# Sparse-expert slots of a fused attention and MoE kernel: who computes the weight splits, who scales the result, and in which order

## The chip, the cores and the metric

The kernel runs on one core of one Trainium2 chip. The metric is the device time of one execution in microseconds (us). TensorE is written PE, its weight loads PEld, VectorE DVE, ScalarE ACT, GpSimd POOL and SyncE SP. A "q" behind a name (POOLq) is that engine's sequencer, which issues DMAs, counts semaphores and branches. SBUF is the on-chip memory, PSUM the memory that PE writes to.

## The reference

Three stages follow one another: a decayed causal attention, a dense mixture of experts (every token through all 8 experts, weighted by a balanced table P), and a sparse mixture (every token through the one expert with the largest logit).

```python
def reference(**kw):
    attn_out = _attn_ref(q, k, v)                       # 4 x 8 heads x 576 x 64
    x = attn_out.transpose(0, 2, 1, 3).reshape(2304, 512)
    x = _moe_ref(x, moe_w_gate, moe_w1, moe_w2)         # dense, E = 8, F = 1024
    return _moe2_ref(x, moe2_w_gate, moe2_w1, moe2_w2)  # sparse

def _moe2_ref(x, w_gate, w1, w2):
    logits = x @ w_gate
    expert_idx = np.argmax(logits, axis=1)
    gate_w = softmax(logits)[np.arange(N), expert_idx]
    for e in range(8):
        mask = expert_idx == e
        h = np.maximum(x[mask] @ w1[e], 0.0)            # w1[e]: 512 x 1024
        out[mask] = gate_w[mask, None] * (h @ w2[e])    # w2[e]: 1024 x 512
```

All is float32. The kernel multiplies on PE in a reduced 32-bit format (fp32r) and keeps accuracy by splitting each operand into a high part `hi` (the value rounded to fp32r) and a low part `lo = value - hi`; one product is then three matmuls: hi·hi, hi·lo and lo·hi.

## The kernel before

Attention takes the first 330 us, the dense experts run until about 1695 us, and the rest is the sparse stage, class `Top1`, which the change is about. It sorts the tokens by expert and works in **slots** of 128 rows of one expert. There are up to 26 slots (NSLOT); 18 of them (NFULL) run always, slots 18 to 25 stand each under its own guard `tc.If(n > t)`. In the profiled execution 22 slots run, 0 to 21, and four guards are skipped. Slots 0 and 1 are woven by hand into the routing arithmetic of `build`; slots 2 to 21 are calls of `slot(t)`, each 48 products of 128x512 columns on PE and three groups of four transposes.

One expert's weights are eight **units** of 128x1024: units 0 to 3 are rows of w1, units 4 to 7 pieces of w2. A unit c lands by an SP transfer of 512 KB in the tile `raws[c]` (only where the next slot's expert differs), and `split(c)` makes its two halves: ACT copies raw to hi (op0h to op6h, u7h), then lo = raw - hi (op0l to op6l, u7l) is computed, for c = 3 and 7 on POOL, for the others on DVE. The split is done anew for every slot, changed expert or not.

The work of a slot t, in the order in which it is written:

- `gather(t + 2)`: POOL fetches 128 rows of a later slot by an indirect DMA into `xg`.
- `hidden(t, 0)` and `hidden(t, 1)`: 12 products each on PE (tile phs) of the row's transposed halves xth, xtl with units 0 to 3; after each, two splits of units 4 to 7 and `relu` on ACT (tile hrow).
- the SP loads of units 4 to 7 for slot t + 1.
- `th(0)`, `tx(t + 1)`, `th(1)`: three groups of four PE transposes in a row. `th` transposes half of the hidden rows (pth; ACT writes hth, DVE htl); `tx` transposes the next slot's token rows (ptx; ACT writes xth, DVE xtl).
- `result`: 24 products (tile pys) of hth and htl with units 4 to 7.
- the splits of units 0, 1, 3, 2 for slot t + 1, and the loads of units 0 to 3 for slot t + 2 (`ahead`).
- `finish`: o = pys * gate on DVE (L1325), then POOL writes the 128 rows to their places in the output by an indirect DMA (L1328).

ACT, DVE and PE run their instructions in the written order; for SP and POOL a scheduler chooses the order. Each engine works through its own queue in order and waits at the head for what its next instruction needs. Two results, o0 and o1 of slots 0 and 1, are kept unscaled (`keep`, L1318) until the gates are known; the function `mid` scales and writes them within slot 2.

Of the kernel before, what the change touches and what calls it, by code (L numbers as in the profile page):

```python
# [15 lines left out]
AF = mybir.ActivationFunctionType  # L16
ALU = mybir.AluOpType
# [20 lines left out]
def split_lo(eng, out, src, hi):  # L38

    return eng.tensor_tensor(out=out, in0=src, in1=hi.bitcast(F32), op=ALU.subtract)  # L40
# [336 lines left out]
def drain(gen):  # L377

    while True:
        try:  # L380
            next(gen)
        except StopIteration as s:
            return s.value
# [95 lines left out]
def token_tasks(nc, X, ops, lo_engs):  # L479
# [18 lines left out]
    def sub(out, a, b):  # L498
# [4 lines left out]
    b11, b12, b21, b22 = (0, 0), (1, 0), (0, 1), (1, 1)  # L503
    return [
        split(B11, *b11), split(B21, *b21), sub(b11, b12, b11),
        sub(b12, b22, b12),
        split(B22, *b22), sub(b22, b22, b11), split(T2, *b22),
        split(T1, *b11), split(T3, *b12), sub(b21, b21, b22), split(T4, *b21),
    ]

# [241 lines left out]
MANUAL = {mybir.EngineType.Activation, mybir.EngineType.DVE, mybir.EngineType.PE}  # L752
NSLOT = 26
NFULL = NT
# [397 lines left out]
class Top1:  # L1152
# [58 lines left out]
    def unit(self, c):  # L1211
        return self.units[c]

    def split(self, c, eng=None):
        hi, lo = self.unit(c)
        self.nc.scalar.activation(hi, self.raws[c], AF.Copy)  # L1216
        if eng is None:
            eng = self.nc.gpsimd if c in (3, 7) else self.nc.vector
        split_lo(eng, lo, self.raws[c], hi)

    def xt(self, t):
        return tuple(x[:, t % 2] for x in self.xts)
# [41 lines left out]
        nc.scalar.activation(hi[:, gs, :], pt, AF.Copy)  # L1264
        split_lo(nc.vector, lo[:, gs, :], pt, hi[:, gs, :])

    def result(self, hi, lo, py=None, gs=range(2)):
        if py is None:
            py = self.pyp.tile([128, DM], F32, name="pys", tag="py")
        n = 12 * gs[0]  # L1270
        for g in gs:
            fcs = range(4 * g, 4 * g + 4)
            w = {fc: [x[:, 512 * (fc % 2):512 * (fc % 2) + 512] for x in self.unit(4 + fc // 2)]
                 for fc in fcs}
            mm = [(hi, fc, w[fc][i]) for fc in fcs for i in range(2)]
            mm += [(lo, fc, w[fc][0]) for fc in fcs]
            for a, fc, ww in mm:
                self.nc.tensor.matmul(py, a[:, fc, :], ww, start=n == 0, stop=n == 23)
                n += 1
        return py  # L1280

    def slot(self, t, mid=None):
        h, hi, lo = self.begin()
        if t + 2 < NSLOT:
            self.gather(t + 2)
        for f in range(2):
            ph = self.hidden(t, f)
            for c in (4 + 2 * f, 5 + 2 * f):
                self.split(c)
            self.relu(f, ph, h)  # L1290
        if t + 1 < NSLOT:
            if t >= NFULL:
                self.regs_of(t + 1)
            for c in range(4, 8):
                self.load(t + 1, c)
        self.th(0, h, hi, lo)
        if t + 1 < NSLOT:
            self.tx(t + 1, self.ptp, "pt")
        self.th(1, h, hi, lo)
        if mid:  # L1300
            mid()
        py = self.result(hi, lo)
        if t + 1 < NSLOT:
            for c in (0, 1, 3, 2):
                self.split(c)
        self.ahead(t + 2)
        self.finish(t, py)

    def ahead(self, t):
        if t < NSLOT:  # L1310
# [10 lines left out]
    def finish(self, t, py, o=None):  # L1321
        nc = self.nc
        if o is None:
            o = self.op.tile([128, DM], F32, name="o", tag="o")
        nc.vector.tensor_scalar(  # L1325
            out=o, in0=py, scalar1=self.res["gate"][:, t:t + 1], scalar2=None, op0=ALU.mult
        )
        nc.gpsimd.indirect_dma_start(  # L1328
            out=self.out,
            out_offset=bass.IndirectOffsetOnAxis(ap=self.res["sidx"][:, t:t + 1], axis=0),  # L1330
            in_=o, in_offset=None, bounds_check=N - 1, oob_is_err=False,
        )
# [3 lines left out]
def build(ctx, tc, q, k, v, moe_w_gate, moe_w1, moe_w2, moe2_w_gate, moe2_w1, moe2_w2,  # L1336
          c_gk, c_gq, c_row, out):
    nc = tc.nc
# [88 lines left out]
    gs = ExitStack()  # L1427
# [24 lines left out]
    with tc.manual_schedule(engines=order):  # L1452
# [3 lines left out]
        for u in range(2 * E):  # L1456
# [20 lines left out]
            if u == 2 * E - 1:  # L1477
# [8 lines left out]
                g, w = nc.gpsimd, nc.vector  # L1486
# [24 lines left out]
        t1 = None  # L1511
        for n, u in enumerate(range(2 * E - 1, -1, -1)):
# [8 lines left out]
            else:  # L1521
# [3 lines left out]
                t1 = Top1(tc, ctx, ident, x2d, moe2_w1, moe2_w2, res, out, list(ops), raws, aux)  # L1525
# [38 lines left out]
    with tc.manual_schedule(engines=MANUAL):  # L1564
        t1.gather(1)
        t1.split(7)
        ro.v.bg = [ro.gates(0, tmp)]
        h0, h1 = t1.begin(), t1.begin()

        ph = t1.hidden(0, 0, None, range(0, 2))  # L1570
        next(lp)
        ph = t1.hidden(0, 0, ph, range(2, 4))
        drain(lp)
        t1.relu(0, ph, h0[0])
        ro.choose(1, tmp)
        ro.v.bg.append(ro.gates(1, tmp))
        ph = t1.hidden(0, 1, None, range(0, 1))
        ro.count(1)
        t1.hidden(0, 1, ph, range(1, 4))
        t1.relu(1, ph, h0[0])  # L1580
        ro.totals(1)
        ro.slots(tmp)
        t1.th(0, *h0)
        t1.th(1, *h0)
        t1.tx(1, t1.ptp, "pt")
        py = t1.result(*h0[1:])
        ro.experts(tmp)
        t1.ahead(2)
        o0 = t1.keep(0, py)

        ro.ranks(1)
        ro.slots_of(tmp)
        ph = t1.hidden(1, 0)
        t1.relu(0, ph, h1[0])
        ph = t1.hidden(1, 1)
        t1.relu(1, ph, h1[0])
        ro.onehot(tmp)
        ro.rows(tmp)
        for t in (2, 3):
            t1.gather(t)  # L1600
        t1.th(0, *h1)
        t1.th(1, *h1)
        for c in range(4):
            t1.split(c)
        py = t1.result(*h1[1:], None, range(0, 1))
        t1.tx(2, t1.ptp, "pt")
        t1.result(*h1[1:], py, range(1, 2))
        for c in range(4, 8):
            t1.load(2, c)
        ro.v.rest()  # L1610
        t1.ahead(3)
        o1 = t1.keep(1, py)
        rg = ro.row_gates(tmp)
        next(rg)

        def mid():
            drain(rg)
            t1.finish(0, o0, o0)
            t1.finish(1, o1, o1)

        for t in range(2, NFULL):
            t1.slot(t, mid if t == 2 else None)
    n = nc.values_load(
        res["nslot"][0:1, 0:1], min_val=NFULL, max_val=NSLOT,
        skip_runtime_bounds_check_because="18 to 26 slots hold 2304 tokens of 8 experts",
    )
    for t in range(NFULL, NSLOT):
        with tc.If(n > t):
            with tc.manual_schedule(engines=MANUAL):
                t1.slot(t)  # L1630


def consts():
# [33 lines left out]
```

## Time and profile before

| | |
|---|---|
| time, median of 3 runs (lowest to highest) | 2002.8 us (2002.36 to 2005.55) |
| the profiled execution's own time | 2002.13 us |
| its span in the trace | 2000.3 us |
| mean granted clock of PE, share of full speed | 0.996 |
| busy share of PE, DVE, ACT, POOL over the span | 98%, 63%, 42%, 15% |
| start of slot 2, start of slot 3, last product of slot 21 | 1725.91, 1738.87, 1986.94 us |

Times in the trace count from the start of the span; 1.8 us of the execution lie outside it. A row of a timeline gives start, duration, engine, line of the kernel, operation, the tile written, the tiles read, the shape, and in brackets how long the engine had been idle before it and what ended that. A product (MATMUL) is listed with 0.39 us, but products overlap: their starts follow one another every 0.23 us.

### The profile page before, as it was taken

The page shows a single profiled execution, that of the slowest core. Times are in us where ns is not written, and L with a number is a line of the kernel's source. Part 1 is how long each engine was busy: PE and PEld are TensorE (multiplying, and loading weights), DVE is VectorE, ACT ScalarE, POOL GpSimd, SP SyncE. Part 2 cuts the span into 40 slices and gives each one's busy share as a digit, 9 for nine tenths or more (in the row PEclk, how much of TensorE's full clock was granted, in tenths as well). Part 3 has the DMA queues.
Part 4 walks back from the last instruction along what each step waited for, and adds up shares of the span by engine and source line. Part 5 has one row for each costly group of instructions (what it writes and reads, how often), then busy time and mean ns, then how long its engine had stood idle before and what let it go on. Part 6 is the DMA issues. An engine that isn't in the chain of part 4 may idle for free.

```text
span 2000.3 us, 25444 instructions
## 1 busy us (share of the span) xinstructions
PE 1956.9 (98%) x9584; PEld 1627.4 (81%) x9584; DVE 1252.1 (63%) x2059; ACT 847.7 (42%) x1454; POOL 298.9 (15%) x250
## 2 busy tenths in 40 slices
PE   8989999999999999999999999999999999999997
PEld 7777888888888888888878888888878888777775
DVE  7897565555555555555455556555576654988886
ACT  6665424232222233323333333333333334577785
POOL 6572000000000000000000000000000001465654
PEclk9999999999999999999999999999999999999998
DMA  5621111111111110111311111111111113112755
GB/s 132 142 61 64 42 43 43 43 43 43 43 42 43 43 37 28 42 43 43 111 33 64 43 43 64 42 54 52 43 46 60 47 59 116 43 43 77 249 200 192
DMA packets 112111, 134.94 MB, mean 67 GB/s; under 512 B 62190, under 2 KB 62446, under 8 KB 111600
## 3 DMA queue, kind: packets, MB, share of 16 engines
q1 hardware_dynamic: 106960, 121.92, 19.0%
q0 software_dynamic: 3680, 11.02, 1.7%
q8 instruction: 77, 1.26, 0.3%
q10 hardware_dynamic: 1344, 0.33, 0.1%
q14 instruction: 50, 0.41, 0.1%
HBM read 182.53 MB, written 12.58 MB: 98 GB/s over the span
## 4 chain that ended last, share of the span: by engine, by line
PE 82%; DVE 8%; ACT 5%; issue 3%; DMA 1%; POOL 0%; SPq 0%; ACTq 0%; POOLq 0%; DVEq 0%
PE pyt L731 37%; PE pha L609 17%; PE phc L609 8%; PE phr L706 5%; PE phb L609 4%; PE phs L1250 4%; DVE op2l L40 2%; PE po L274 2%; PE ps L210 1%; ACT op3h L1216 1%; PE pS L236 1%; ACT op2h L1216 1%; PE rpl L832 1%; DMA raw<-in_moe_w_dram 1%; PE pgate L1381 1%
## 5 line engine op out<-in xcount | busy, mean ns | idle before, releaser
L731 PE MATMUL pyt<-w2hi,hhi 128*128 128x512 f32 x1024 | 402.5, 393 | 2.4 <-DVE xb L742 2.2
L731 PE MATMUL pyt<-w2hi,hlo 128*128 128x512 f32 x1024 | 398.9, 390 | 0.0
L731 PE MATMUL pyt<-w2lo,hhi 128*128 128x512 f32 x1024 | 398.5, 389 | 0.0
L635 ACT ACTIVATE q<-pha 128x512 f32<-128x512 f32 x192 | 114.7, 599 | 266.8 <-PE pha L609 264.4
L623 ACT ACTIVATE hhi<-q 128x512 fp32r<-128x512 f32 x192 | 121.4, 632 | 249.9 <-DVE q L631 249.9
L731 PEld LDWEIGHTS pyt<-w2hi,hhi 128*128 128x128 f32 x1024 | 192.3, 188 | 42.8 <-DVE xb L742 2.9
L731 PEld LDWEIGHTS pyt<-w2hi,hlo 128*128 128x128 f32 x1024 | 192.2, 188 | 40.7
L731 PEld LDWEIGHTS pyt<-w2lo,hhi 128*128 128x128 f32 x1024 | 192.4, 188 | 38.8
L624 DVE SCALAR_TENSOR_TENSOR hlo<-q,hhi 128x512 fp32r<-128x512 f32 x192 | 133.0, 693 | 96.8 <-ACT hhi L623 90.8
L742 DVE SCALAR_TENSOR_TENSOR xa<-pyt,P,xa 128x512 f32<-128x512 f32 x140 | 105.0, 750 | 136.0 <-PE pyt L731 135.2
L742 DVE SCALAR_TENSOR_TENSOR xb<-pyt,P,xb 128x512 f32<-128x512 f32 x120 | 90.1, 751 | 94.0 <-PE pyt L731 94.0
L631 DVE TENSOR_TENSOR q<-phb,q 128x512 f32<-128x512 f32 x64 | 44.3, 692 | 166.0 <-PE phb L609 166.0
L40 POOL TENSOR_TENSOR op2l<-xb,op2h 128x1024 fp32r<-128x1024 f32 x1 | 2.4, 2387 | 719.4 <-ACT op2h L494 719.4
L631 DVE TENSOR_TENSOR q<-phc,q 128x512 f32<-128x512 f32 x128 | 87.8, 686 | 34.0 <-PE phc L609 33.1
L561 ACT ACTIVATE w3h<-raw 128x512 fp32r<-128x512 f32 x31 | 19.6, 631 | 160.4 <-DVE raw L567 160.3
L567 DVE TENSOR_TENSOR raw<-raw 128x512 f32<-128x512 f32 x124 | 85.1, 687 | 1.1
L40 DVE TENSOR_TENSOR w2lo<-raw,w2hi 128x512 fp32r<-128x512 f32 x124 | 84.6, 683 | 0.0
L587 ACT ACTIVATE w2hi<-raw 128x512 fp32r<-128x512 f32 x124 | 77.1, 623 | 0.0
L714 DVE SCALAR_TENSOR_TENSOR rlo<-phr,rhi 128x512 fp32r<-128x512 f32 x32 | 22.1, 691 | 87.7 <-ACT rhi L713 87.7
L908 POOL TENSOR_SCALAR Bm<-c,ro 128x128 bf16<-128x128 bf16 x2 | 1.3, 653 | 456.2 <-DVE ro L408 456.2
L561 ACT ACTIVATE w4h<-raw 128x512 fp32r<-128x512 f32 x31 | 19.6, 632 | 116.2 <-DVE raw L567 116.2
L40 DVE TENSOR_TENSOR op2l<-raw,op2h 128x1024 fp32r<-128x1024 f32 x22 | 60.6, 2756 | 10.1 <-ACT op2h L1216 9.6
(391 smaller groups left out, 4765.3 us busy)
## 6 DMA issues: line engine op xcount, KB each, us to landing
raw<-in_moe_w_dram SPq DMA_DIRECT2D x180, 512.0 KB
raw<-in_moe_w_dram SPq DMA_DIRECT2D x62, 1024.0 KB
kt<-in_k_dram SPq DMA_DIRECT2D x32, 128.0 KB
vt<-in_v_dram SPq DMA_DIRECT2D x32, 128.0 KB
qt<-in_q_dram SPq DMA_DIRECT2D x32, 128.0 KB
x2d<-xa SPq DMA_DIRECT2D x10, 256.0 KB
xbd<-xb SPq DMA_DIRECT2D x1, 2048.0 KB
xb<-xbd SPq DMA_DIRECT2D x2, 1024.0 KB
```

The source lines that it names most:

```text
L40: return eng.tensor_tensor(out=out, in0=src, in1=hi.bitcast(F32), op=ALU.subtract)
L567: nc.vector.tensor_tensor(out=q(*out), in0=q(*a), in1=q(*b), op=op)
L587: nc.scalar.activation(hi, self.raw2[:, fc, :], AF.Copy)
L609: self.nc.tensor.matmul(bank, ww[:, k, 128 * p:128 * p + 128], xx[:, k, :], start=start and n == 0, stop=stop and n == 5, skip_group_check ...
L623: nc.scalar.activation(hi, c, AF.Relu)
L624: nc.vector.scalar_tensor_tensor(out=lo, in0=c, scalar=0.0, in1=hi.bitcast(F32), op0=ALU.max, op1=ALU.subtract)
L631: self.nc.vector.tensor_tensor(out=s, in0=p, in1=s, op=ALU.add)
L635: self.nc.scalar.activation(t, c, AF.Copy)
L706: nc.tensor.matmul(pt[:, j, :], w[:, k, 128 * j:128 * j + 128], xr[x][:, xi, k, :], start=n == 0, stop=n == 11,)
L731: nc.tensor.matmul(pt, hh, ww, start=n == 0, stop=n == 11)
L742: nc.vector.scalar_tensor_tensor(out=acc, in0=pt, scalar=P[:, i, e:e + 1], in1=acc, op0=ALU.mult, op1=ALU.add)
L1250: nc.tensor.matmul(ph, xx[:, k, :], ww[:, fs], start=n == 0, stop=n == 11)
```

## The change

Five things are changed, all in the sparse stage.

1. The low halves of all eight units are computed on DVE; POOL computes none.
2. `finish` scales on ACT instead of DVE, for o0 and o1 in slot 2 as well.
3. `slot` is written in another order: the transposes are spread among the products (th(0) in the middle of the second hidden half, tx behind it, th(1) after eight result products), the splits of units 0 to 5 for the next slot are spread over the slot, and the splits of units 6 and 7 open the next one. The loads follow: 4 and 5 at the slot's start, 6 and 7 behind their splits.
4. In `build`, the loads of units 4 to 7 for slot 2 and its splits 4 and 5 stand earlier.
5. The guards of slots 18 to 25 are nested: the guard of slot t + 1 stands inside the body of slot t.

```diff
-    def split(self, c, eng=None):
+    def split(self, c):
         hi, lo = self.unit(c)
         self.nc.scalar.activation(hi, self.raws[c], AF.Copy)
-        if eng is None:
-            eng = self.nc.gpsimd if c in (3, 7) else self.nc.vector
-        split_lo(eng, lo, self.raws[c], hi)
+        split_lo(self.nc.vector, lo, self.raws[c], hi)
...
     def slot(self, t, mid=None):
         h, hi, lo = self.begin()
+        nxt = t + 1 < NSLOT
         if t + 2 < NSLOT:
             self.gather(t + 2)
-        for f in range(2):
-            ph = self.hidden(t, f)
-            for c in (4 + 2 * f, 5 + 2 * f):
-                self.split(c)
-            self.relu(f, ph, h)
-        if t + 1 < NSLOT:
+        if nxt:
             if t >= NFULL:
                 self.regs_of(t + 1)
-            for c in range(4, 8):
+            for c in (4, 5):
                 self.load(t + 1, c)
+        ph = self.hidden(t, 0)
+        for c in (6, 7):
+            self.split(c)
+            if nxt:
+                self.load(t + 1, c)
+        self.relu(0, ph, h)
+        ph = self.hidden(t, 1, None, range(0, 2))
+        if nxt:
+            self.split(0)
         self.th(0, h, hi, lo)
-        if t + 1 < NSLOT:
+        self.hidden(t, 1, ph, range(2, 4))
+        if nxt:
+            self.split(1)
+        self.relu(1, ph, h)
+        if nxt:
+            self.split(2)
             self.tx(t + 1, self.ptp, "pt")
+        py = self.result(hi, lo, None, slice(0, 8))
         self.th(1, h, hi, lo)
         if mid:
             mid()
-        py = self.result(hi, lo)
-        if t + 1 < NSLOT:
-            for c in (0, 1, 3, 2):
-                self.split(c)
+        if nxt:
+            self.split(3)
+        self.result(hi, lo, py, slice(8, 24))
+        if nxt:
+            self.split(4)
+            self.split(5)
+        self.finish(t, py)
         self.ahead(t + 2)
-        self.finish(t, py)
...
-        nc.vector.tensor_scalar(
-            out=o, in0=py, scalar1=self.res["gate"][:, t:t + 1], scalar2=None, op0=ALU.mult
-        )
+        nc.scalar.activation(o, py, AF.Copy, scale=self.res["gate"][:, t:t + 1])
...
         t1.ahead(2)
+        for c in range(4, 8):
+            t1.load(2, c)
         o0 = t1.keep(0, py)
...
-        py = t1.result(*h1[1:], None, range(0, 1))
+        py = t1.result(*h1[1:], None, slice(0, 12))
+        t1.split(4)
         t1.tx(2, t1.ptp, "pt")
-        t1.result(*h1[1:], py, range(1, 2))
-        for c in range(4, 8):
-            t1.load(2, c)
+        t1.result(*h1[1:], py, slice(12, 24))
+        t1.split(5)
...
-    for t in range(NFULL, NSLOT):
-        with tc.If(n > t):
-            with tc.manual_schedule(engines=MANUAL):
-                t1.slot(t)
+    def further(t):
+        if t < NSLOT:
+            with tc.If(n > t):
+                with tc.manual_schedule(engines=MANUAL):
+                    t1.slot(t)
+                further(t + 1)
+
+    further(NFULL)
```

On DVE one whole slot reads as follows before, from the split of unit 6 on (raw_101 to raw_13812 are the tiles of the landed weights, two units in each of the first two):

```order
L40 TENSOR_TENSOR op6l<-raw_13811,op6h 128x1024
L40 TENSOR_TENSOR htl<-pth,hth 128x512
L40 TENSOR_TENSOR xtl<-ptx,xth 128x512
L40 TENSOR_TENSOR htl<-pth,hth 128x512
L40 TENSOR_TENSOR op0l<-raw_101,op0h 128x1024
L40 TENSOR_TENSOR op1l<-raw_101,op1h 128x1024
L40 TENSOR_TENSOR op2l<-raw_102,op2h 128x1024
L1325 TENSOR_SCALAR o<-pys,gate 128x512
L40 TENSOR_TENSOR op4l<-raw_13809,op4h 128x1024
L40 TENSOR_TENSOR op5l<-raw_13810,op5h 128x1024
```

and this is the same stretch of DVE's queue with the change:

```order
L40 TENSOR_TENSOR op6l<-raw_13811,op6h 128x1024
L40 TENSOR_TENSOR u7l<-raw_13812,u7h 128x1024
L40 TENSOR_TENSOR op0l<-raw_101,op0h 128x1024
L40 TENSOR_TENSOR htl<-pth,hth 128x512
L40 TENSOR_TENSOR op1l<-raw_101,op1h 128x1024
L40 TENSOR_TENSOR op2l<-raw_102,op2h 128x1024
L40 TENSOR_TENSOR xtl<-ptx,xth 128x512
L40 TENSOR_TENSOR htl<-pth,hth 128x512
L40 TENSOR_TENSOR op3l<-raw_102,op3h 128x1024
L40 TENSOR_TENSOR op4l<-raw_13809,op4h 128x1024
L40 TENSOR_TENSOR op5l<-raw_13810,op5h 128x1024
```

The two splits of POOL have come in, the scaling of the result has gone, and the splits now stand between the small ones.

On PE, this is the passage from the hidden products to the result products of one slot before:

```order
L1250 MATMUL phs<-op3h,xtl 128x512
L1262 MATMUL pth<-ident,hrow 128x128 x4
L1229 MATMUL ptx<-ident,xg_13815 128x128 x4
L1262 MATMUL pth<-ident,hrow 128x128 x4
L1278 MATMUL pys<-op4h,hth 128x512
```

and with the change, from the middle of the second hidden half to the ninth result product:

```order
L1248 MATMUL phs<-op1h,xtl 128x512
L1260 MATMUL pth<-ident,hrow 128x128 x4
L1248 MATMUL phs<-op2h,xth 128x512
L1248 MATMUL phs<-op2l,xth 128x512
L1248 MATMUL phs<-op2h,xtl 128x512
L1248 MATMUL phs<-op3h,xth 128x512
L1248 MATMUL phs<-op3l,xth 128x512
L1248 MATMUL phs<-op3h,xtl 128x512
L1227 MATMUL ptx<-ident,xg_13815 128x128 x4
```

The three groups of transposes stood together and now stand apart, each behind products; the third (second half of the hidden rows) follows eight result products further on.

On POOL the queue ends before with these instructions for the last guard (the ISA row counts up the semaphores of the slot's transfers where the slot is skipped):

```order
L1628 COMPARE_AND_BRANCH
L40 TENSOR_TENSOR u7l<-raw_13812,u7h 128x1024
L1328 DMA out_dram<-o,sidx 2304x512
L1628 UNCONDITIONAL_BRANCH
L1628 ISA
L1628 UNCONDITIONAL_BRANCH
```

and with the change with these:

```order
L1642 COMPARE_AND_BRANCH
L1339 DMA out_dram<-o,sidx 2304x512
L1642 COMPARE_AND_BRANCH
L1339 DMA out_dram<-o,sidx 2304x512
L1642 UNCONDITIONAL_BRANCH
L1642 ISA
L1642 UNCONDITIONAL_BRANCH
L1642 ISA
```

A skipped guard was followed by the next guard, with an ISA row of its own for each; now the skipped branches stand one behind the other at the end of the program, each followed by a jump past the rest, so that one of them is run.

## Rows read from the trace of the kernel before

**Rows 1.** Busy us by window: span, PE, PEld, DVE, ACT, POOL, PEclk, DMA share, GB/s.

```profile
1940.00:1960.00 20.00, 19.67 (x98) 16.05 (x97) 16.86 (x17) 17.27 (x23) 12.01 (x7) 1.00 0.95 329
```

**Rows 2.** Chain that ended last, two steps: start, duration, engine, tile, line.

```profile
1921.31 2.89 DVE op2l L40
...
1934.32 2.88 DVE op2l L40
```

**Rows 3.** Waits from 1720 us on: total us, times, longest us.

```profile
PE phs L1250 <- DVE op2l L40: 7.5, 19, 1.2
...
ACT op5h L1216 <- DMA raw<-in_moe_w_dram: 2.0, 3, 1.0
```

**Rows 4.** Timeline at the start of slot 14, PE, DVE and POOL.

```profile
1881.38 2.68 POOL L40 TENSOR_TENSOR op3l<-raw,op3h 128x1024 fp32r<-128x1024 f32 x1 [1.41 <-ACT op3h L1216]
...
1882.28 2.88 DVE L40 TENSOR_TENSOR op2l<-raw,op2h 128x1024 fp32r<-128x1024 f32 x1 [0.48 <-ACT op2h L1216]
...
1884.48 0.39 PE L1250 MATMUL phs<-op2h,xth 128*128 128x512 f32 x1
...
1885.21 0.50 PE L1250 MATMUL phs<-op2l,xth 128*128 128x512 f32 x1 [0.34 <-DVE op2l L40]
...
1885.54 0.39 PE L1250 MATMUL phs<-op2h,xtl 128*128 128x512 f32 x1
...
1885.77 0.40 PE L1250 MATMUL phs<-op3h,xth 128*128 128x512 f32 x1
```

**Rows 5.** Timeline of the same slot: two groups of transposes, ACT's copy of the first.

```profile
1889.20 0.60 PE L1262 MATMUL pth<-ident,hrow 128*128 128x128 f32 x4
...
1889.64 0.60 PE L1229 MATMUL ptx<-ident,xg 128*128 128x128 f32 x4
...
1889.89 0.59 ACT L1264 ACTIVATE hth<-pth 128x512 fp32r<-128x512 f32 x1
```

**Rows 6.** Timeline of slot 17: ACT and DVE.

```profile
1931.48 1.23 DVE L40 TENSOR_TENSOR op0l<-raw,op0h 128x1024 fp32r<-128x1024 f32 x1
1932.26 1.08 ACT L1216 ACTIVATE op3h<-raw 128x1024 fp32r<-128x1024 f32 x1
1932.62 1.22 DVE L40 TENSOR_TENSOR op1l<-raw,op1h 128x1024 fp32r<-128x1024 f32 x1
1933.21 1.08 ACT L1216 ACTIVATE op2h<-raw 128x1024 fp32r<-128x1024 f32 x1
```

**Rows 7.** Timeline of slot 18: a split and POOL's output transfer beside it.

```profile
1937.78 1.21 DVE L40 TENSOR_TENSOR op4l<-raw,op4h 128x1024 fp32r<-128x1024 f32 x1
1938.13 1.72 POOL L1328 DMA_INDIRECT out_dram<-o,sidx  x1 [2.02 <-DVE o L1325]
```

**Rows 8.** Timeline of the end of slot 1 and of slot 2: DVE and PE.

```profile
1724.11 0.68 DVE L40 TENSOR_TENSOR xtl<-ptx,xth 128x512 fp32r<-128x512 f32 x1
...
1726.36 0.39 PE L1250 MATMUL phs<-op0h,xtl 128*128 128x512 f32 x1
...
1734.96 0.20 DVE L408 TENSOR_TENSOR gate<-r_gz 128x26 f32<-128x26 f32 x1
```

**Rows 9.** Timeline of the end: last split, last products, scaling, output.

```profile
1986.32 2.84 DVE L40 TENSOR_TENSOR op2l<-raw,op2h 128x1024 fp32r<-128x1024 f32 x1 [0.48 <-ACTq L1628]
1986.71 0.61 PE L1278 MATMUL pys<-u7h,htl 128*128 128x512 f32 x2
1989.09 0.74 DVE L1325 TENSOR_SCALAR o<-pys,gate 128x512 f32<-128x512 f32 x1
1990.11 1.01 POOL L1328 DMA_INDIRECT out_dram<-o,sidx  x1 [2.03 <-DVEq L1628]
```

**Rows 10.** POOL's sequencer behind it: times, ns min/median/max, first and last start.

```profile
L1628 POOLq INC_SWDGE_SEM  x4: 1055/1058/1115, 1990.4 to 1994.6; - x4
...
L1663 POOLq DRAIN  x3: 52/107/3827, 1995.7 to 2000.1; - x3
```

**Rows 11.** GB/s moved, 1930 to 1990 us in 40 equal slices.

```profile
GB/s 406 411 385 395 384 153 377 356 158 195 335 365 376 422 416 410 361 242 298 318 326 377 429 391 388 343 186 358 373 400 176 12 19 44 167 5 11 0 0 11
```

More of the change, by code (lines that the diff above doesn't have):

```diff
@@ L1265, in th, with result @@
         split_lo(nc.vector, lo[:, gs, :], pt, hi[:, gs, :])
-    def result(self, hi, lo, py=None, gs=range(2)):
+    def result(self, hi, lo, py=None, part=slice(0, 24)):
         if py is None:
             py = self.pyp.tile([128, DM], F32, name="pys", tag="py")
-        n = 12 * gs[0]
-        for g in gs:
+        mm = []
+        for g in range(2):
             fcs = range(4 * g, 4 * g + 4)
@@ L1274, in result @@
                  for fc in fcs}
-            mm = [(hi, fc, w[fc][i]) for fc in fcs for i in range(2)]
+            mm += [(hi, fc, w[fc][i]) for fc in fcs for i in range(2)]
             mm += [(lo, fc, w[fc][0]) for fc in fcs]
-            for a, fc, ww in mm:
-                self.nc.tensor.matmul(py, a[:, fc, :], ww, start=n == 0, stop=n == 23)
-                n += 1
+        for n in range(24)[part]:
+            a, fc, ww = mm[n]
+            self.nc.tensor.matmul(py, a[:, fc, :], ww, start=n == 0, stop=n == 23)
         return py
```

## The prediction

> **What bounds the kernel now.** I read first the windows of the sparse stage: PE is busy 19.67 of 20 us at the full granted clock, DVE 16.86, ACT 17.27 [rows 1]. So the sparse stage is PE's, but not wholly: about 0.3 us in 20 are open, and more is hidden in products that start late. The chain of waits names the place. From slot 3 on it runs through one DVE instruction per slot, op2l, at intervals of 13.01 us [rows 2], and the list of waits has PE waiting for it 19 times, once in each of the slots 3 to 21 [rows 3]. The timeline shows what one such wait costs. op2l lasts 2.88 us where a split beside an idle POOL lasts 1.22; POOL's op3l runs over the same time, 2.68 us [rows 4]. Products start every 0.23 us (1885.54 to 1885.77), but op2h·xth, op2l·xth and op2h·xtl start 0.73 and 0.33 us apart: (0.73 - 0.23) + (0.33 - 0.23) = 0.60 us lost per slot [rows 4]. The rest of a slot is fixed work of PE: 48 products by 0.23 us and three groups of transposes at 0.44 us (1889.20 to 1889.64 [rows 5]): 11.04 + 1.32 = 12.4 us. With the loss that is 13.0, the interval that the chain shows. So a slot without the loss takes 12.4 us.
>
> After the last product there is a tail in which PE does nothing. The last pair of products starts at 1986.71, but the scaling on DVE starts only at 1989.09, because op2l of a slot that never runs stands ahead of it until 1989.16 [rows 9]. POOL's transfer starts at 1990.11, and then POOL's sequencer counts semaphores for the four skipped slots, 1.06 us each and 1.4 apart (1990.4 to 1994.6), before it drains [rows 10].
>
> **The change part by part.**
>
> *All splits on DVE.* POOL no longer runs beside DVE, so each of the eight splits should take the pitch 1.14 us (1931.48 to 1932.62 [rows 6]). Per slot DVE then has 8 x 1.14 + 3 x 0.68 [rows 8] = 11.2 us of work, ACT 8 x 0.95 (1932.26 to 1933.21) + 6 x 0.60 [rows 5, 6] = 11.2 us: both below 12.4. What held PE, a split that lasts 2.88 us and comes late, is gone; in the new order the last units needed by the next slot's first half, 2 and 3, are written before the result products end, so next late would be op3l, needed 9 products (2.1 us) into the slot. The loss goes in 18 slots by 0.60. In one it was larger: the longest wait is 1.2 us against the 0.34 of slot 14 [rows 3, 4], so 0.60 + 0.86 = 1.46. Together 18 x 0.60 + 1.46 = **-12.3 us**. From below it is bounded by the waiting that is listed, 7.5 us [rows 3], which leaves out what PE's weight loads waited ahead of it; from above by 14, if a slot comes down to 12.3 as rounding of the pitch allows.
>
> A page's rule speaks against this: the Trainium skill, "SBUF — State Buffer", section "Who interferes with whom", says that a VectorE instruction with two SBUF inputs contends with a GpSimd instruction that reads SBUF, the loser standing still for the whole of the other. The rows on op2l and op3l agree with it. Were POOL's output transfer such an instruction, the change would lose by it, since DVE now has two-input splits in flight most of the time; that is the rival "POOL holds DVE" below. The row is against it: op4l lasts 1.21 us with the transfer beside it from 1938.13 on, and it is the transfer that is stretched, to 1.72 from 1.01 alone [rows 7, 9].
>
> *The transposes apart.* Each group was followed at 0.44 us by the next [rows 5]; apart they cost that once each at least to 0.35 at best, so between -0.3 and +0.1 per slot; I take 0, the row. The new places change who must be in time. With the slot's first product at T, th(0) stands at T + 4.1 (18 products), when relu0, freed at T + 2.8, is long done if ACT is not behind. th(1) stands 8 products behind tx, at about T + 8.2. hth of it is copied 0.69 us after its start and lasts 0.59 [rows 5], so it is there at T + 9.5; the first product that reads it is the 13th of the result, at 8.2 + 0.44 + 4 x 0.23 = T + 9.55. That is a margin of a few hundredths: it is a rival below.
>
> *Slots 1 and 2.* Two terms are losses. xtl of slot 2 ran at 1724.11 to 1724.79 and was needed at 1726.36 [rows 8]. In DVE's new order op3l and op4l come before it: 2 x 1.14 us later, so it ends at 1727.07, **+0.7** (0 if PE loses nothing because DVE gets there earlier, 2.3 if both splits count in full). In slot 2, o0 and o1 now stand on ACT ahead of the splits of units 3, 4, 5 and all behind them, and wait for the gate, which DVE writes at 1734.96 after the second hth [rows 8]. With th(1) at T + 8.2, that gate is there at about T + 11; then o0, o1, 3h, 4h, 5h, o, 6h, 7h and relu0 follow on ACT, 5 x 0.95 + 4 x 0.5 = 6.8 us, so relu0 ends at T + 17.8, while PE wants it for th(0) of slot 3 at T + 13.0 (this slot's length before, with the gate's products in it) + 4.1 = 17.1: **+1.0**, since DVE's op3l may delay the gate a little more (0 to 4.4, the latter if the gate comes 3 us later).
>
> *Scaling on ACT.* One small ACT instruction more per slot is in the 11.2 above, and DVE is rid of one. At the end it counts: ACT's queue ends with that scaling where DVE's op2l stood in its way; it can start when the last product is done, whose group ends at 1986.71 + 0.61 = 1987.32 [rows 9], so at about 1987.4 instead of 1989.09: **-1.7** (0 to -1.8). POOL's transfers and the end behind it move along.
>
> *Nested guards.* One skipped branch remains of four, so three times 1.4 us of counting go: **-4.2** [rows 10]. The drain behind lasts up to 3.83 us [rows 10]; if it waits for the output transfer itself and not for the counting, the end stays tied to that and the gain is 0; if it waits for what the counting left behind, it shrinks with it, to -7. I take the middle, the counting alone.
>
> *Loads.* In each slot with a new expert eight transfers of 0.52 MB and the gathered and written rows pass, 4.72 MB. At the mean of the window, 329 GB/s at a busy share of 0.95 [rows 1], the full rate would be 346, or 13.6 us a slot, more than 12.4. But the tiles are free early: unit 0's is split by about T + 5.7 and its next copy comes 3.4 us into the next slot, 10 us later, for a transfer that at 346 GB/s takes 1.5 us alone and 3 with another beside it (an estimate), so some 7 us are slack; and slices at 406 to 429 GB/s [rows 11] say that the engines can do more. ACT already waits for loads of unit 5 three times, 2.0 us in all [rows 3]. I put **+0.5** (0 to 3.7).
>
> *Sum.* -12.3 + 0.7 + 1.0 + 0.5 - 1.7 - 4.2 = -16.0. From the profiled execution's 2002.1 that is 1986.1; its median of three stands 0.7 above, so against the median 1986.8. I take **1986.4**.
>
> **The rivals.**
>
> *The loads take over.* In the last four slots, each with a new expert, 13.6 us instead of 12.4: 4 x 1.2 = 4.8 us beside the sum's 0.5: 1991. It decides once the transfers fall behind by more than the slack of 7 us. For it: the waits of [rows 3]; against it the slices above 400 GB/s [rows 11].
>
> By a page: the Trainium skill, "DMA: Bandwidth & Descriptors", section "Specifications", gives about 358 GB/s as one core's limit from HBM. By it a slot's loads take 13.2 us (an estimate from that figure), and the four slots lose 3.6. The trace does not agree with it as a ceiling: slices of 1.5 us stand at 406 to 429 GB/s [rows 11].
>
> *th(1) is late.* If its margin is negative by 0.2 us, as by one queueing of hth behind another ACT copy of 0.95 us every fifth time or a little each slot, 20 x 0.2 = 4: 1990.5.
>
> *The change does not do what it says at the end.* If the drain is tied to the output transfer, the 4.2 stay: 1990.6.
>
> *POOL holds DVE (slower).* If each of POOL's two transfers per slot, the gather and the output, stops DVE for its whole length, at most 2 x 1.72 us [rows 7] and at least 2 x 1.01 [rows 9], say 2.7, DVE needs 11.2 + 2.7 = 13.9 us a slot against 13.0: 20 x 0.9 = 18, less the tail's 5.9, gives 2014. It decides from 13.3 us of DVE per slot on, where the loss passes the gain at the end. Against it stands [rows 7]; for it only that DVE's idle time, which hid such things, is nearly used up.
>
> **How the numbers follow.** My forecast, 1982 to 1989.5, has a chance of 0.57; the loads 0.14; th(1) 0.11; the drain 0.09; POOL holds DVE 0.04. Of the 0.05 left, 0.03 are several of these at once, 0.02 gains of more than I summed. The first four lie between 1982 and 1993, so the range is **1981.5 to 1993**. A measurement of this kernel can tell 0.2%, 4 us, from no change: that is below 1998.8 or above 2006.8. Each of the first four alone is faster; two at once reach 1996, three are the same, for which I put the 0.03. Faster 0.93, same 0.03, slower 0.04.
>
> **What would show it.** In the new trace each split on DVE at 1.2 us, none at 2.9; phs waiting no more for op2l; intervals of 12.3 to 12.4 us between slots; one wait of 0.5 to 1.5 us for xtl in slot 2 and one of PE for hrow at the start of slot 3; the scaling within 1 us of the last product; one INC_SWDGE_SEM. Intervals at 12.6 with hth waited for speak for th(1); the last four slots longer than the others, with waits of ACT for raw, for the loads; splits beside DMA_INDIRECT at over 1.5 us for POOL. Wrong altogether it would be if slots came at 13 us again with DVE or ACT busy throughout: then the work of either is more than 11.2 us.

## The result and the profile after

The changed kernel takes **1985.9 us** (median of 4 runs, 1985.58 to 1988.5) against 2002.58 before: ratio 0.9907, 95% interval 0.9892 to 0.9921. The prediction was 1986.4, faster, in a range of 1981.5 to 1993. Its profiled execution took 1985.58 us, span 1983.9; before it was 2002.13 and 2000.3, so 16.4 us went from the span. I ask where each of them went, and whether for the reason that I gave.

The window of the sparse stage (columns as in [rows 1]) now has PE busy throughout, at the full granted clock:

```profile
1940.00:1960.00 20.00, 20.00 (x100) 16.39 (x99) 18.01 (x18) 18.49 (x24) 5.09 (x4) 1.00 1.01 362
```

The waits from 1720 us on (columns as in [rows 3]) have lost the line of PE's products on op2l that stood there 19 times. The longest of what PE or its loads wait for now are these; but for the first, each comes once:

```profile
PEld pys L1278 <- ACT hth L1262: 4.2, 20, 0.5
...
PEld pth L1260 <- ACT hrow L1253: 1.5, 1, 1.5
...
PE pth L1260 <- ACT hrow L1253: 1.1, 1, 1.1
PE ptx L1227 <- DMA xg<-x2d,gidx: 0.8, 1, 0.8
...
PEld phs L1248 <- DVE xtl L40: 0.6, 1, 0.6
```

The groups between 1740 and 1975 us (instruction and count, busy us and mean ns of one, idle time before) show DVE's splits at 1.22 us, op2l among them, which was 2.88 [rows 4]; POOL's gathers are what has grown, from 1.10 to 1.70 us:

```profile
L1181 POOL DMA_INDIRECT xg<-x2d,gidx x17 | 29.0, 1703 | 54.2 <-PE ptx L1227 53.0 <-issue 1.2
...
L40 DVE TENSOR_TENSOR op2l<-raw,op2h 128x1024 fp32r<-128x1024 f32 x19 | 23.3, 1225 | 1.6
...
L40 DVE TENSOR_TENSOR op4l<-raw,op4h 128x1024 fp32r<-128x1024 f32 x19 | 23.2, 1219 | 0.0
```

Slots 5 to 21 start 12.35 us apart in the mean (before 13.01). The start of slot 14, which [rows 4] shows of before, has its products at 0.23 us:

```profile
1877.68 0.39 PE L1248 MATMUL phs<-op0h,xth 128*128 128x512 f32 x1
...
1877.90 0.39 PE L1248 MATMUL phs<-op0l,xth 128*128 128x512 f32 x1
...
1879.04 0.39 PE L1248 MATMUL phs<-op2h,xth 128*128 128x512 f32 x1
1879.27 0.39 PE L1248 MATMUL phs<-op2l,xth 128*128 128x512 f32 x1
...
1879.49 0.39 PE L1248 MATMUL phs<-op2h,xtl 128*128 128x512 f32 x1
```

The end, to be laid beside [rows 9] and [rows 10]: the scaling starts 0.65 us after the last pair of products (before 2.38), and one counting instruction is left.

```profile
1976.05 0.62 PE L1278 MATMUL pys<-u7h,htl 128*128 128x512 f32 x2
1976.70 0.69 ACT L1338 ACTIVATE o<-pys,gate 128x512 f32<-128x512 f32 x1 [0.30 <-PE pys L1278]
...
1977.67 1.24 POOL L1339 DMA_INDIRECT out_dram<-o,sidx  x1 [9.53 <-ACTq L1642]
```

```profile
L1642 POOLq INC_SWDGE_SEM  x1: 1128/1128/1128, 1977.9 to 1977.9; - x1
...
L1680 POOLq DRAIN  x3: 52/107/3827, 1979.2 to 1983.6; - x3
```

The passage into slots 2 and 3 is where time was lost (beside [rows 8]): the transposes of slot 2's rows wait for the gather, the third product of slot 2 waits for xtl, and at the start of slot 3 the transposes wait for hrow.

```profile
1723.81 0.63 PE L1227 MATMUL ptx<-ident,xg 128*128 128x128 f32 x4 [0.80 <-DMA xg<-x2d,gidx]
...
1727.05 0.68 DVE L40 TENSOR_TENSOR xtl<-ptx,xth 128x512 fp32r<-128x512 f32 x1
...
1727.27 0.39 PE L1248 MATMUL phs<-op0l,xth 128*128 128x512 f32 x1
...
1727.79 0.50 PE L1248 MATMUL phs<-op0h,xtl 128*128 128x512 f32 x1
```

```profile
1745.82 0.66 PE L1260 MATMUL pth<-ident,hrow 128*128 128x128 f32 x4 [1.10 <-ACT hrow L1253]
```

### The profile page after: what moved, and what is told of

It reads as the page before. It is cut to its first block, busy times and chain, and to the rows that moved or that the text cites. A ratio compares the mean times of both kernels' runs of the same rounds, so it can differ in the third digit from the quotient of the medians.

```text
span 1983.9 us, 25329 instructions
## 1 busy us (share of the span) xinstructions
PE 1954.4 (99%) x9584; PEld 1628.8 (82%) x9584; DVE 1251.8 (63%) x2082; ACT 867.8 (44%) x1478; POOL 190.4 (10%) x207
## 4 chain that ended last, share of the span: by engine, by line
PE 79%; issue 9%; DVE 6%; POOL 2%; DMA 2%; ACT 1%; SPq 0%; POOLq 0%; ACTq 0%; DVEq 0%
PE pyt L731 38%; PE pha L609 17%; PE phc L609 8%; PE phr L706 5%; PE phb L609 4%; PE po L274 2%; DMA out_dram<-o,sidx 1%; PE ps L210 1%; POOL xg L1181 1%; POOL out_dram L1339 1%; PE pS L236 1%; PE rpl L832 1%; PE pgate L1392 1%; DVE vlo L33 0%; DVE qbd L40 0%
## 5 line engine op out<-in xcount | busy, mean ns | idle before, releaser
L1181 POOL DMA_INDIRECT xg<-x2d,gidx x24 | 39.0, 1627 | 303.2 <-PE phc L609 186.6
L224 POOL TENSOR_SCALAR_AFFINE_SELECT s<-s 128x512 fp32r<-128x512 f32 (+1 forms) x96 | 50.3, 562 | 46.0 <-DVE s L40 46.0
```

The costliest lines, as they stand in the source:

```text
L1181: self.nc.gpsimd.indirect_dma_start(out=self.xg[t % 3], out_offset=None, in_=self.x2d[0:rows, :], in_offset=bass.IndirectOffsetOnAxis(ap=i ...
```

## The experiments

From each run's trace I read, beside the time, the starts of the slots' first products. The stages ahead of the slots end up to 5 us earlier or later from one execution to the next, and from slot 0 to slot 1 some traces take 22.8 us, others (e2, e5, e6, e8 and e9) 24.35, whether or not their code of that passage differs; these distances leave both out:

| run | median us | slot 2 to 3 | slot 3 to 4 | slots 5 to 21, mean | start of slot 21 to end of span |
|---|---|---|---|---|---|
| before | 2002.58 | 12.96 | 13.88 | 13.01 | 26.13 |
| after | 1985.9 | 13.43 | 13.70 | 12.35 | 19.78 |
| e1_flat | 1990.65 | 13.47 | 13.62 | 12.35 | 23.37 |
| e2_pool37 | 1999.76 | 17.66 | 14.99 | 12.54 | 22.20 |
| e3_old_dve8 | 1989.62 | 12.96 | 12.76 | 12.35 | 24.12 |
| e4_mid_dve | 1985.76 | 13.39 | 13.24 | 12.34 | 20.01 |
| e5_o_dve | 1986.83 | 13.48 | 13.23 | 12.36 | 21.10 |
| e6_loads | 1993.72 | 13.04 | 13.42 | 12.35 | 21.44 |
| e8_th1 | 1996.3 | 13.57 | 14.20 | 12.79 | 20.14 |
| e9_old_order | 1986.43 | 12.96 | 12.79 | 12.36 | 19.69 |
| e7_both | 1985.89 | 13.24 | 12.35 | 12.35 | 19.90 |
| f1_after | 1985.73 | 13.40 | 13.64 | 12.34 | 19.75 |
| f2_both | 1983.67 | 13.15 | 12.35 | 12.35 | 19.84 |

My theory: the pace of the slots comes from taking POOL's splits away, the end from the scaling on ACT and from the nesting, and the rewritten order adds nothing of its own. The rival: it is the order that makes the pace.

**Splits or order?** Two kernels, each with one of the two.

```diff
 e3_old_dve8, against the kernel before
-            eng = self.nc.gpsimd if c in (3, 7) else self.nc.vector
+            eng = self.nc.vector
 e2_pool37, against the changed kernel
-        split_lo(self.nc.vector, lo, self.raws[c], hi)
+        split_lo(self.nc.gpsimd if c in (3, 7) else self.nc.vector, lo, self.raws[c], hi)
```

> The kernel before with one line changed: all eight low halves on DVE, the old order, scaling on DVE, guards side by side. Theory 'engines': slots 12.4 us apart instead of 13.0, -12 us, and the last scaling 1 us earlier because op2l ahead of it takes 1.2 instead of 2.8: about 1989.5. Theory 'order': DVE's eight splits in a row come too late for the next slot, 13.0 us or more, 2001 to 2010.

> The changed kernel with the low halves of units 3 and 7 on POOL again, in the new order. Theory 'engines' (POOL's splits hold a DVE split up, and that is what cost 0.6 us a slot): two DVE splits per slot near 2.9 us again, DVE at 12.3 us of work per slot and late, slots 12.6 to 13.0 us apart, 1991 to 1999. Theory 'order' (the new order puts each split so early that a slow one harms nobody): slots still 12.35 us apart, 1986.

The one-line change brings 1989.62 (ratio 0.9923, 0.9900 to 0.9946), with every slot from 4 on 12.35 us long in the old order. Its timeline has the splits of units 0, 1, 3 and 2 on DVE one behind the other, op3l and op2l at 1.22 us each:

```profile
1898.49 1.22 DVE L40 TENSOR_TENSOR op1l<-raw,op1h 128x1024 fp32r<-128x1024 f32 x1
...
1899.63 1.22 DVE L40 TENSOR_TENSOR op3l<-raw,op3h 128x1024 fp32r<-128x1024 f32 x1
...
1900.76 1.22 DVE L40 TENSOR_TENSOR op2l<-raw,op2h 128x1024 fp32r<-128x1024 f32 x1
```

So the splits alone are enough for the pace. But the order alone is nearly enough, too, which I had not expected: with POOL's splits back, slots 5 to 17 come 12.39 us apart. DVE's splits are stretched as before, only now none that is urgent:

```profile
1821.31 2.41 POOL L40 TENSOR_TENSOR op3l<-raw,op3h 128x1024 fp32r<-128x1024 f32 x1 [2.40 <-ACT op3h L1216]
...
1822.20 2.60 DVE L40 TENSOR_TENSOR op4l<-raw,op4h 128x1024 fp32r<-128x1024 f32 x1
```

What this kernel loses, it loses where something more comes in. In slot 2 it is xtl, for which PE waits 2.8 us, among others. From slot 18 on slots take 13.1 to 13.5 us. It is not the loading of weights that makes the difference: slot 13 moves as much as slot 19 (345 and 347 GB/s) and takes 12.40 us against 13.07.

```profile
1872.74:1885.14 12.40, 12.40 (x61) 10.05 (x60) 11.45 (x10) 11.15 (x14) 8.32 (x5) 1.00 0.97 345
...
1948.14:1961.21 13.07, 12.66 (x62) 10.03 (x60) 11.66 (x10) 11.14 (x14) 7.87 (x4) 1.00 0.99 347
```

What is new from slot 18 on is the guard, and with it the order of POOL's queue. Without a guard u7l comes first and the gather behind it, as in slot 15; under a guard the gather stands ahead of u7l, as in slots 18 and 19. So u7l starts 4.8 and 4.4 us after the slot's first product instead of 2.9, op0l lasts 3.59 and 3.19 us beside it instead of 2.5, and the two htl that PE wants stand behind op0l on DVE:

```profile
1900.41 3.27 POOL L40 TENSOR_TENSOR u7l<-raw,u7h 128x1024 fp32r<-128x1024 f32 x1 [0.39 <-ACT u7h L1216]
...
1904.32 1.36 POOL L1181 DMA_INDIRECT xg<-x2d,gidx  x1 [0.65 <-PE ptx L1227]
...
1937.30 1.21 DVE L40 TENSOR_TENSOR op6l<-raw,op6h 128x1024 fp32r<-128x1024 f32 x1
...
1937.42 2.01 POOL L1181 DMA_INDIRECT xg<-x2d,gidx  x1 [0.30 <-issue]
...
1939.38 3.59 DVE L40 TENSOR_TENSOR op0l<-raw,op0h 128x1024 fp32r<-128x1024 f32 x1 [0.86 <-ACT op0h L1216]
...
1939.46 2.42 POOL L40 TENSOR_TENSOR u7l<-raw,u7h 128x1024 fp32r<-128x1024 f32 x1
...
1942.89 0.68 DVE L40 TENSOR_TENSOR htl<-pth,hth 128x512 fp32r<-128x512 f32 x1
...
1947.09 0.74 PE L1278 MATMUL pys<-op6h,htl 128*128 128x512 f32 x2 [0.48 <-DVE htl L40]
...
1951.50 1.03 POOL L1181 DMA_INDIRECT xg<-x2d,gidx  x1 [0.30 <-issue]
...
1952.56 2.40 POOL L40 TENSOR_TENSOR u7l<-raw,u7h 128x1024 fp32r<-128x1024 f32 x1
```

That the order of POOL's queue costs these slots their 0.7 to 1.1 us is read from the trace; no run changed that order alone.

The two edits remove the same loss, once by its cause and once by its urgency; their gains do not add. Neither theory was whole.

**The old order with the rest of the change.** The kernel before with all splits on DVE, the scaling of slots 2 and on on ACT, nested guards.

```diff
-        nc.vector.tensor_scalar(
-            out=o, in0=py, scalar1=self.res["gate"][:, t:t + 1], scalar2=None, op0=ALU.mult
-        )
+        if t < 2:
+            nc.vector.tensor_scalar(
+                out=o, in0=py, scalar1=self.res["gate"][:, t:t + 1], scalar2=None, op0=ALU.mult
+            )
+        else:
+            nc.scalar.activation(o, py, AF.Copy, scale=self.res["gate"][:, t:t + 1])
...
+                further(t + 1)
```

> The kernel before, in its old order, with three parts of the change: all low halves on DVE, the scaling of slots 2 and on on ACT (o0 and o1 stay on DVE), nested guards. Theory (the new order adds nothing to the slots' pace and costs something in slots 2 and 3): slots 12.35 us apart, slots 2 and 3 as in the one-line run (12.96, 12.76), the end 19.8 us behind the start of slot 21: 1984.3, faster than the changed kernel by 1.5. Rival (the order pays, by putting ACT's scaling where it harms nobody; in the old order it holds op4h up): slots over 12.4 us apart, 1987 or more.

Measured 1986.43 (1984.37 to 1988.79), between the two expected times. The slots do as the theory says, slots 2 and 3 are 1.4 us shorter together than in the changed kernel, and the end is 0.1 shorter. The time does not show it: in the profiled execution slot 2 started 1.4 us later against slot 0 than in the one-line run, which has the same code there. That the new order earns nothing in the pace is shown; that it costs 1.5 us in the time is not.

**The end.** The changed kernel with guards side by side, and the changed kernel with the scaling of slots 2 and on back on DVE.

```diff
 e1_flat
-    def further(t):
-        if t < NSLOT:
-            with tc.If(n > t):
-                with tc.manual_schedule(engines=MANUAL):
-                    t1.slot(t)
-                further(t + 1)
-
-    further(NFULL)
+    for t in range(NFULL, NSLOT):
+        with tc.If(n > t):
+            with tc.manual_schedule(engines=MANUAL):
+                t1.slot(t)
 e5_o_dve
-        nc.scalar.activation(o, py, AF.Copy, scale=self.res["gate"][:, t:t + 1])
+        if t >= 2:
+            nc.vector.tensor_scalar(
+                out=o, in0=py, scalar1=self.res["gate"][:, t:t + 1], scalar2=None, op0=ALU.mult
+            )
+        else:
+            nc.scalar.activation(o, py, AF.Copy, scale=self.res["gate"][:, t:t + 1])
```

> The changed kernel with the guards side by side again, nothing else. My theory (the end follows POOL's counting): four INC_SWDGE_SEM at 1.4 us apart instead of one, so +4.2 us, about 1990.1, slots still 12.35 us apart, the last product at the same time. Rival (the end is tied to the last output transfer, the counting is hidden): no change, 1985.9, with the last drain shorter.

> The changed kernel with the scaling of slots 2 and on back on DVE (o0 and o1 stay on ACT). Theory (ACT has the scaling only for the end's sake): slots still 12.35 us apart, since DVE then has 11.9 us of work per slot; at the end the splits 4 and 5 of a slot that never runs stand ahead of it on DVE, so it starts 1.3 us later: +1.3, 1987.2. Rival (DVE at 11.9 of 12.35 us falls behind): slots 12.5 us apart or more, 1990.

Flat guards put the end 3.6 us later (23.37 against 19.78), not 4.2: the four countings follow at 1.3 us, and the drain behind them is as long as ever, 3.83 us. So the end follows the counting, and the nesting is worth 3.6.

```profile
L1641 POOLq INC_SWDGE_SEM  x4: 1055/1058/1115, 1978.1 to 1982.0; - x4
...
L1676 POOLq DRAIN  x3: 52/107/3827, 1983.1 to 1987.5; - x3
```

With the scaling on DVE it starts 1.93 us after the last pair of products instead of 0.65, behind op5l of a slot that never runs; that is 1.28 us, and the end comes 1.3 later. The slots stay at 12.36 us with DVE busy for 18.9 to 19.4 of 20 us: even that much work on DVE doesn't slow PE.

```profile
1978.40 0.61 PE L1278 MATMUL pys<-u7h,htl 128*128 128x512 f32 x2
...
1979.20 1.22 DVE L40 TENSOR_TENSOR op5l<-raw,op5h 128x1024 fp32r<-128x1024 f32 x1
...
1980.33 0.74 DVE L1339 TENSOR_SCALAR o<-pys,gate 128x512 f32<-128x512 f32 x1
```

**The loads.** Every slot loads its weights anew.

```diff
         ev, ch = self.regs[t]
+        ch = None
```

> The changed kernel with the weights loaded anew in every slot, changed expert or not (4.2 MB of loads and 0.5 MB of rows per slot). If the transfers sustain only the 362 GB/s that the window of slots 18 and 19 shows at a busy share of 1.0, a slot's transfers take 13.0 us: the slots come 13.0 us apart once the slack of some 7 us is used up, 1990 to 1998, with ACT waiting for raw. If that window was full only because of what was asked, and the rate goes to the 410 GB/s of its best slices: slots stay at 12.35, 1986.

Slots at 12.35 us from slot 4 to the end, with no wait of ACT for raw, while the transfers move 380 GB/s over the 200 us from 1760 on (334 to 400 in windows of 20 us); two windows of its trace:

```profile
1780.00:1800.00 20.00, 20.00 (x97) 16.34 (x96) 18.34 (x19) 17.69 (x23) 5.07 (x4) 1.00 1.04 396
...
1860.00:1880.00 20.00, 20.00 (x101) 16.51 (x100) 18.05 (x19) 17.89 (x24) 5.89 (x4) 1.00 0.99 368
```

So the loads bound nothing in these slots, though in the changed kernel's window of slots 19 and 20 the busy share already stood at 1.0 with 362 GB/s. The median of 1993.72 fits the theory that saw the slots at 13.0 us, but the 7.8 us that this kernel takes more lie elsewhere. In the traces 5.3 come ahead of slot 3, of which 2.8 are a longer wait of slot 2's transposes for the gathered rows (3.6 us instead of 0.8) and 1.6 the longer passage from slot 0 to 1 that traces without these loads have as well; 1.7 come from slot 21 to the end. Why the gathered rows land so late was not tested.

**The third group of transposes.** Moved from the 9th to the 11th place of the result.

```diff
-        py = self.result(hi, lo, None, slice(0, 8))
+        py = self.result(hi, lo, None, slice(0, 10))
...
-        self.result(hi, lo, py, slice(8, 24))
+        self.result(hi, lo, py, slice(10, 24))
```

> The changed kernel with the third group of transposes two products later (after 10 instead of 8 of the result). If its margin is as thin as the timeline says (hth ready 1.3 us after the group's start, read 0.44 + 4 x 0.23 after it), taking 0.46 us from it costs about 0.45 us in each of 20 slots: 12.8 us apart, 1995. If there is slack that the timeline hides, 12.35 and 1986.

12.79 us a slot, +0.44, and 1996.3: of the 0.46 us by which the group was moved 0.44 are lost, so the margin is as thin as it was worked out. The place behind nine products was not tried. PE's loads wait for hth 12.3 us in all instead of 4.2:

```profile
PEld pys L1278 <- ACT hth L1262: 12.3, 19, 0.7
```

**Slots 1 to 3.** First only o0 and o1 back on DVE:

```diff
-        nc.scalar.activation(o, py, AF.Copy, scale=self.res["gate"][:, t:t + 1])
+        if t < 2:
+            nc.vector.tensor_scalar(
+                out=o, in0=py, scalar1=self.res["gate"][:, t:t + 1], scalar2=None, op0=ALU.mult
+            )
+        else:
+            nc.scalar.activation(o, py, AF.Copy, scale=self.res["gate"][:, t:t + 1])
```

> The changed kernel with only the two kept results o0 and o1 scaled on DVE instead of ACT. Theory (ACT's queue waits for the gate there, and relu0 of slot 3 behind it holds PE): the step from slot 3 to slot 4 comes down from 13.70 to 12.4 us, 1984.6. Rival (ACT is behind there whatever stands in its queue): the wait for hrow stays, 1985.9.

Only 0.46 of the 1.35 us came, and the time (1985.76) does not show it. ACT no longer waits for the gate, but at its next scaling for an output tile: there are two, and the one it needs is still being written out. relu0 is late as before.

```profile
1742.53 0.69 ACT L1343 ACTIVATE o<-pys,gate 128x512 f32<-128x512 f32 x1 [2.52 <-DMA out_dram<-o,sidx]
...
1745.65 0.66 PE L1260 MATMUL pth<-ident,hrow 128*128 128x128 f32 x4 [0.67 <-ACT hrow L1253]
```

Then a third output tile beside it, and slot 2's transposes later and ahead of split 4 (run twice, the second time beside the changed kernel itself):

```diff
-        self.op = ctx.enter_context(tc.tile_pool(name="c_o", reuse_waits="tile", bufs=2))
+        self.op = ctx.enter_context(tc.tile_pool(name="c_o", reuse_waits="tile", bufs=3))
...
-        py = t1.result(*h1[1:], None, slice(0, 12))
-        t1.split(4)
+        py = t1.result(*h1[1:], None, slice(0, 16))
         t1.tx(2, t1.ptp, "pt")
-        t1.result(*h1[1:], py, slice(12, 24))
+        t1.split(4)
+        t1.result(*h1[1:], py, slice(16, 24))
```

> The changed kernel with o0 and o1 on DVE, three output tiles o instead of two, and in slot 1 the transposes of slot 2's rows after 16 instead of 12 result products and ahead of split 4. Theory (three waits cost the changed kernel what its slots 2 and 3 are longer: transposes for the gathered rows 0.8, xtl 0.4, the output tile and relu0 1.3): slot 3 comes down from 13.70 to 12.4, slot 2 from 13.43 to 13.0, slot 2 starts 0.8 earlier against slot 1: 1983.4. Rival (one of them is hidden behind another): 1984.5 to 1985.9.

> The changed kernel once more, to be set beside the next run on the same chip. 1986 at the median; the sparse stage, from its first product to the end of the span, 295.6 us as in its first trace, or up to 1.5 more where the routing arithmetic ahead of slot 2 waits longer.

> The changed kernel with three waits of slots 1 to 3 taken away (o0 and o1 scaled on DVE, three output tiles, slot 2's transposes after 16 result products and ahead of split 4), once more. In its first trace the sparse stage took 293.2 us against 295.6, while the stages ahead of it took 4.5 us longer than usual. If those 4.5 us are chance: 1983.5 at the median, 2.4 below the changed kernel on the same chip. If the rewritten code brings them about: the sparse stage starts late again and the two medians agree.

The first run (e7_both) gave 1985.89, from 1982.88 to 1988.03, with slots 2 and 3 at 13.24 and 12.35 but the whole sparse stage 4.5 us later. In the second, with the same code, the stage begins at 1687.93 us, where it began before (1687.65), so the code doesn't bring the 4.5 us about: 1983.67 (1982.8 to 1986.91) against 1985.73 (1985.04 to 1987.95) for the changed kernel on the same chip. Of the ten executions of this version in both runs six lie below all nine of the changed kernel, the other four between 1985.89 and 1988.03. The wait for hrow is gone:

```profile
1741.91 0.60 ACT L1253 ACTIVATE hrow<-phs 128x512 f32<-128x512 f32 x1 [0.19 <-PE phs L1248]
...
1743.02 0.60 PE L1260 MATMUL pth<-ident,hrow 128*128 128x128 f32 x4
```

The sparse stage, from its first product to the end of the span, takes 293.2 us in both its traces, 295.6 and 295.3 in those of the changed kernel, 312.7 before. This version is the fastest here, 2.1 us ahead of the changed kernel by the medians. What the third tile and the later transposes bring each for itself was not run.

## Why the prediction was right, step by step

- **What bounded the kernel** was read rightly: op2l, held up by POOL's op3l, once per slot. Taking only that away (e3_old_dve8) brings the slots to 12.35 us.
- **The loss per slot** was put at 0.60 us and 12.3 in all. It measured 0.66 in slots 5 to 20, 0.61 in slot 21, 0.91 in slot 4, and 1.53 in slot 3, read from f2_both where nothing else delays that slot. That is 16 x 0.66 + 0.61 + 0.91 + 1.53 = 13.6: the term was too small by 1.3. The gaps of two products that I added up were most of it, but not all; the distance between slots was the better measure, had I not rounded 11.04 + 1.32 = 12.36 up to 12.4.
- **The transposes apart** were put at nothing, and that held: the one-line run has them together and its slots take 12.35 us as well.
- **Engines' work** at 11.2 us for ACT and DVE held, and with room.
- **xtl of slot 2** was to end at 1727.07 and ended at 1727.73 (1727.05 + 0.68). The sparse stage begins 0.70 us later in this trace, so against its first product xtl came as predicted. PE lost 0.4 and not 0.7 by it, because slot 2 itself began later.
- **relu0 of slot 3** was put at +1.0 and cost 1.35. Taking the gate from ACT's queue gave back 0.46 of that; behind it stood the output tile that frees late, which I had not seen (e4_mid_dve).
- **Not foreseen**: slot 2's transposes waited 0.8 us for the gathered rows instead of 0.4.
- **The scaling at the end**: -1.7 predicted, 2.38 - 0.65 = 1.73 measured, and 1.3 when ACT's share alone was undone in the new order.
- **The nested guards**: -4.2 predicted, 3.6 measured (e1_flat). Of the three cases the middle one is true: the drain keeps its 3.83 us and follows the counting. From the first count to the drain it took 5.3 us before [rows 10], 5.0 with flat guards in e1_flat and 1.3 now, so 4.0 went. The 0.3 beside the nesting come with the splits that POOL no longer has: the one-line run takes 5.0, too.

```profile
L1628 POOLq INC_SWDGE_SEM  x4: 1055/1058/1115, 1977.2 to 1981.1; - x4
...
L1663 POOLq DRAIN  x3: 52/107/3827, 1982.2 to 1986.6; - x3
```

- **The loads**: +0.5 predicted, nothing found; slots 18 to 20 are 12.35 us long as well. So are slots 13 and 17 with 362 and 337 GB/s: weights are loaded there too, which the prediction, with only the last four slots in view, left out. In its second working of that rival four slots at 13.2 instead of 12.4 us lose 3.2, not 3.6.

From the sparse stage 17.1 us went: -13.6 + 1.35 for slot 3, +0.9 up to the start of slot 3 (gathered rows 0.4, slot 2 longer by 0.5), -1.7 for the scaling, -3.6 for the nesting, -0.3 for the rest of the counting, and some 0.1 that I cannot name. The stages ahead took 0.7 us longer in the one trace. That the sum of -16.0 came so near was in part chance: a loss put too small and losses and gains put too large made up for one another.

Of the rivals, *the loads take over* falls with e6_loads, *the change does not do what it says at the end* with e1_flat, *POOL holds DVE* with the splits at 1.22 us beside transfers of 1.7. *th(1) is late* was a true danger: its margin is spent to the last hundredths, as e8_th1 shows (0.44 us lost of 0.46). What the prediction did not say is that the new order was not needed for the pace.

## What to carry to other kernels

If an engine is late because another holds it up, there are two cures, to move the other's work or to make the late result less urgent; ask what each brings alone before both are credited. Work out where the last result comes from and what stands ahead of it in its engine's queue: a scaling moved to the engine that had nothing left ahead of it, and one skipped branch counted instead of four, were worth a third of this gain. When a wait is taken away, look for the next one behind the same instruction, such as the number of output tiles.

## What the runs showed of the hardware that was not expected

The busy share of the DMA engines is no measure of what is left: it stood at 1.01 with 362 GB/s in the changed kernel and at 1.04 with 396 GB/s in e6_loads, and the slots there stayed at 12.35 us.

A split on DVE and one on POOL hold each other up. In e2_pool37 from slot 5 on DVE's take up to 3.59 us beside POOL's, where DVE alone takes 1.22; POOL's u7l takes 2.4 us where no split is running on DVE when it starts (slots 19 to 21), and 3.25 where one began 0.2 us earlier (slots 5 to 17). The Trainium skill, "SBUF — State Buffer", section "Who interferes with whom", states that a VectorE instruction with two SBUF inputs contends with a GpSimd instruction that reads SBUF. Both splits are of that kind, each reads raw and a high half, and these times agree.

POOL's indirect transfers do not slow the splits, which stay at 1.22 us beside them; they are themselves held up. Where no split runs when a transfer starts it takes 1.0 us; in the changed kernel from slot 5 on it takes 0.9 us more than that split still has to run, 1.78 us with 0.86 left:

```profile
1884.11 1.22 DVE L40 TENSOR_TENSOR op1l<-raw,op1h 128x1024 fp32r<-128x1024 f32 x1
...
1884.47 1.78 POOL L1181 DMA_INDIRECT xg<-x2d,gidx  x1 [4.34 <-PE ptx L1227]
```

In slot 18 of e2_pool37 it is 2.01 with 1.09 left. The loads have no part in it: with loads in every slot the gather takes the same 1.78 us (e6_loads).
